# A head's hash beside the FFN: two matmul passes into two single banks instead of three, the low rows added on VectorE

## The chip, the cores and the metric

The kernel runs on one core of a Trainium2 chip. The metric is the device time of one execution in microseconds (us). Lower is better. Before the change three runs gave 966.29, 969.30 and 969.34 us, median 969.30 us.

## The reference

Attention in which a query sees only the keys of its own hash bucket, followed by a feed-forward network (FFN). Four batches, eight heads, 768 positions, 64 numbers to a head; the FFN goes from 512 to 2048 and back to 512.

```python
q_bits = (np.einsum('bhsd,dk->bhsk', q, proj) > 0)        # 6 bits
k_bits = (np.einsum('bhsd,dk->bhsk', k, proj) > 0)
mask = q_bucket[:, :, :, None] == k_bucket[:, :, None, :]  # buckets: the bits as a number
scores = np.where(mask, scale * q @ k.T, -1e9)
attn = softmax(scores)
x = (attn @ v)  as (B*S, H*D)
h = x @ w_in
out = (h * np.clip(h + 3, 0, 6) / 6) @ w_out
```

The sign of the projections must come out as in float32, so the kernel keeps each operand as a high part, rounded to TensorE's fp32r format, and a low part, the rest.

## The kernel before, in words

Work is cut into 192 steps, numbered `k` in the code: 32 heads times 6 blocks of 128 queries. Each step makes the scores of one block against all 768 keys, takes the row minimum (`lowest`, L396 on VectorE), the exponential (`exponential`, L408 on ScalarE), transposes the result, splits it into high and low (`split_p`, L475 on ScalarE and L479 on VectorE or L477 on GpSimd), and multiplies it with the values (`values_whole`, L514).

From step 101 of 192 on (`beside_ffn`) each step also carries a slice of the FFN: `gemm1` (L664), the gate (L686 ScalarE, L687 VectorE), the split of the gate into `gb` high (L692 ScalarE) and low (L693 VectorE), and `gemm2` (L702, L703 with the high part, L707 with the low one). In that stretch the flag `paced` is set, blocks are transposed by VectorE in 32x32 squares (L429) and by a round trip through DRAM (`flip` writes `fd`, `move` reads it back into the tiles `spare` and `px`, four DMAs a block). When the attention's steps are over, the rest of the FFN runs alone.

The order on TensorE, VectorE, ScalarE and GpSimd is that in which the code is written (`manual_schedule`); every engine takes its queue strictly in order. SyncE (SP), which issues nearly all DMAs, is ordered by the framework's scheduler.

Once a head, every sixth step, the next head is hashed. `split_qk` holds four 128-row tiles: `q1` (query high, key high), `k2` (key low, key high), `q2` (query high, query low) and `k1` (key high, and 12 rows for the bits). `hash_qk` multiplies them with the projection, `bits` turns the signs of 12 query rows and 12 key rows into large numbers that make the scores' mask, and a DMA carries the key rows into `k1`. The hash's output `z` lies in two PSUM banks taken from the four single ones (tags `pt` and `pu`, two buffers each), which `gemm1`, the value products and the small transposes `rt` share. A bank is free again when its readers are done. `raw` (one buffer) receives the next head's queries and keys from DRAM; its key rows come by a DMA of their own (`get_k_rows`). 18 heads are hashed before `paced` is set and 14 after.

Of the kernel before, what the change touches and what calls it, by code (L numbers as in the profile page):

```python
# [10 lines left out]
F32 = mybir.dt.float32  # L11
# [32 lines left out]
def lsh_attention_moe(  # L44
# [31 lines left out]
    def dma(out: bass.AP, in_: bass.AP):  # L76
        nonlocal last
        last = nc.sync.dma_start(out=out, in_=in_)
# [38 lines left out]


    pjl = cp.tile([P, ZM], F32R, name="pjl")
    pjh = cp.tile([P, ZM + ZK - D], F32R, name="pjh")  # L120
    nc.vector.memset(pjl[:].bitcast(F32), 0.0)
    nc.vector.memset(pjh[:].bitcast(F32), 0.0)
    pjk, pjq = pjh[:, :ZM], pjh[:, ZK - D :]


    nc.vector.memset(thr[:], 0.0)
    nc.vector.memset(val[:], 0.0)
    for r, one, big in ((D, 0, -BIG), (ZK, 1, 1.0)):
# [3 lines left out]
        nc.vector.memset(val[r : r + 2 * NB], big * (1, -1)[1 - one])  # L132
        nc.vector.memset(val[r : r + NB], big * (1, -1)[one])
    nc.vector.memset(three[:], 3.0)

    raw0 = sp.tile([P, S], F32, name="raw0", tag="raw", bufs=1)[:]
    dma(out=raw0, in_=qkT[0, 0])
# [117 lines left out]
    def hash_weights():  # L255
        for x in range(2):
            c = ZK + (1 - x) * NB
            nc.vector.tensor_scalar_mul(pjh[:, c : c + NB], pr[:], (1.0, -1.0)[x])
        for r, c in ((slice(0, D), D), (slice(D, P), ZK)):
            pos = pjh[r, ZK + NB : ZM]  # L260
            nc.vector.tensor_sub(pjl[r, c + NB : c + 2 * NB], pr[r], pos.bitcast(F32))
            nc.vector.tensor_sub(pjl[r, c : c + NB], pos.bitcast(F32), pr[r])

    def spans(i: int):

# [11 lines left out]

    copied = None
    subs = []
    moves = []  # L280

    def split_qk(i: int, copy):
        nonlocal copied
# [41 lines left out]
    def hash_qk(i: int):  # L325
        k1, k2, q1, q2 = state[i]
        if paced:
            z = zs[i] = [bank([P, HW], f"z{i}_{j}") for j in range(2)]
        else:
            both = pair(f"z{i}")  # L330
            z = zs[i] = [both[:, j, :HW] for j in range(2)]
        for j in range(2):
            c = slice(j * HW, (j + 1) * HW)
            nc.tensor.matmul(z[j][:ZM], lhsT=pjl[:], rhs=q1[:, c], start=True, stop=False)
            nc.tensor.matmul(z[j][:ZM], lhsT=pjk, rhs=k2[:, c], start=False, stop=False)
            nc.tensor.matmul(z[j][:ZM], lhsT=pjq, rhs=q2[:, c], start=False, stop=True)  # L336
        if not paced:
            zs[i] = both

    def bits(i: int):  # L340
        k1, k2, q1, q2 = state[i]
        z = zs.pop(i)

        if isinstance(z, list):
            whole = [(slice(j * HW, (j + 1) * HW), z[j][D:ZM], False) for j in range(2)]
        elif i == 0:
# [694 lines left out]
    def lead(j: int):  # L1041
# [71 lines left out]
    with tc.manual_schedule(engines={ET.PE, ET.DVE, ET.Activation, ET.Pool}):  # L1113
# [15 lines left out]
        def beside_ffn(k: int):  # L1129
# [81 lines left out]
        for k in range(NS + LT + 2):  # L1211
# [132 lines left out]
```

## Time and profile before

| | us |
|---|---|
| median of three runs | 969.30 |
| the profiled execution | 969.05 |
| its span, first to last instruction | 967.3 |
| TensorE busy | 945.9 |
| VectorE, ScalarE, GpSimd busy | 722.2, 623.5, 474.4 |
| mean granted TensorE clock | 0.999 |

The profiled execution is 1.75 us longer than its span and 0.25 us under the median. "PE" is TensorE's matmuls, "PEld" its weight loads, DVE VectorE, ACT ScalarE, POOL GpSimd, SPq the DMA issues of SyncE. A row of the timeline has: start in us, duration in us, engine, line of the kernel, operation, tile written, tiles read, shape, how many were merged, and in brackets how long the engine had been idle and what released it. A row of the groups has: line, engine, operation, tiles, shape, how many, busy us in all, mean ns of one, idle us before them. "Late" and "slack" below are differences between such rows.

### The profile page before, as it was taken

Reading aid. Unit: us, or ns where it says so; the run is one execution under the profiler, and the core shown is the slowest. Engines: PE = TensorE matmul, PEld = TensorE weight load, DVE = VectorE, ACT = ScalarE, POOL = GpSimd, SP = SyncE. Lnnn points to the kernel's source line nnn. Section 1 sums busy time; section 2 is a strip of 40 time slices with the busy share of each in tenths; the row PEclk is TensorE's granted clock in tenths of the full one; section 3 lists DMA queues with packets and bytes.
Section 4 is the critical chain, followed back from the end, with each engine's and each line's share of the span. In section 5 each row is a group of like instructions: output and inputs, shape, how many; then the busy total and the mean of one; then the engine's idle time right before and its main releaser. Section 6 shows DMA issues by size and latency. Waiting matters only on the chain.

```text
span 967.3 us, 19453 instructions
## 1 busy us (share of the span) xinstructions
PE 945.9 (98%) x6306; PEld 871.8 (90%) x6306; DVE 722.2 (75%) x1470; ACT 623.5 (64%) x1421; POOL 474.4 (49%) x582
## 2 busy tenths in 40 slices
PE   8999999999999999899999999999999999999997
PEld 6999888999989999799999898989999999899996
DVE  7999988888559999778878878878878874342422
ACT  6898876666468888576766766666766664333332
POOL 6777744666537766455555556546546532000000
PEclk9999999999999999999999999999999999999999
DMA  3567579100034454688898788798887782101000
GB/s 113 143 155 188 134 222 375 65 1 1 6 118 118 111 137 123 181 242 243 241 267 234 233 257 249 234 264 237 250 254 232 218 239 68 44 1 44 1 22 22
DMA packets 113613, 152.06 MB, mean 157 GB/s; under 512 B 13876, under 2 KB 82612, under 8 KB 113512
## 3 DMA queue, kind: packets, MB, share of 16 engines
q1 hardware_dynamic: 108472, 144.79, 49.0%
q0 software_dynamic: 5040, 6.03, 5.3%
q8 instruction: 50, 0.82, 0.4%
q14 instruction: 51, 0.42, 0.2%
HBM read 77.34 MB, written 54.00 MB: 136 GB/s over the span
## 4 chain that ended last, share of the span: by engine, by line
PE 83%; DVE 8%; DMA 4%; issue 2%; ACT 2%; POOL 1%; SPq 1%; DVEq 0%; ACTq 0%; POOLq 0%
PE h L664 26%; PE po L702 7%; PE po L707 7%; PE po L703 7%; PE acc L500 6%; PE acc L514 6%; PE s L389 5%; PE s L387 5%; PE pt L418 5%; DVE p L396 2%; DVE pl L479 2%; DMA fd<-p 1%; DVE qq L352 1%; PE rt L590 1%; PE z L336 1%
## 5 line engine op out<-in xcount | busy, mean ns | idle before, releaser
L408 ACT ACTIVATE p<-p,m 128x768 f32<-128x768 f32 x192 | 180.1, 938 | 114.4 <-DVE p L396 100.4
L396 DVE TENSOR_SCALAR_CACHE_REDUCE p<-s 128x768 f32<-128x768 f32 x192 | 182.3, 950 | 18.7 <-PE pt L418 11.7
L687 DVE SCALAR_TENSOR_TENSOR h<-g,h 128x256 f32<-128x256 f32 x192 | 80.8, 421 | 103.7 <-ACT g L686 101.3
L686 ACT ACTIVATE g<-h,three 128x256 f32<-128x256 f32 x192 | 91.0, 474 | 91.0 <-PE h L664 90.6
L664 PE MATMUL h<-xh,w 128*128 128x256 f32 x1024 | 147.3, 283 | 0.8 <-DVE qq L352 0.4
L664 PEld LDWEIGHTS h<-xh,w 128*128 128x128 f32 x1024 | 136.6, 188 | 5.5 <-DVE qq L352 1.7
L429 DVE STREAM_TRANSPOSE p<-p 128x768 f32<-128x768 f32 x90 | 88.1, 978 | 65.5 <-ACT p L408 65.5
L477 POOL TENSOR_TENSOR pl<-spare,ph 128x384 fp32r<-128x384 f32 x45 | 45.8, 1017 | 130.8 <-ACT ph L475 77.9
L479 DVE TENSOR_TENSOR pl<-pt,ph 128x384 fp32r<-128x384 f32 x196 | 100.0, 550 | 3.9 <-ACT ph L475 3.5
L387 PE MATMUL s<-kk,qq 76*128 76x384 f32 x384 | 100.1, 341 | 2.0 <-ACT kk L357 1.5
L389 PE MATMUL s<-kk,qq 128*128 128x384 f32 x384 | 100.3, 342 | 0.0
L702 PE MATMUL po<-w,gb 128*128 128x512 f32 x250 | 98.9, 396 | 0.7 <-ACT gb L692 0.7
L703 PE MATMUL po<-w,gb 128*128 128x512 f32 x250 | 98.6, 394 | 0.0
L475 ACT CAST ph<-pt 128x384 fp32r<-128x384 f32 x196 | 86.0, 473 | 14.7 <-PE pt L418 13.4
L216 POOL TENSOR_TENSOR w<-wr,w 128x128 fp32r<-128x128 f32 x128 | 71.8, 593 | 45.3 <-ACT w L210 41.4
L418 PE MATMUL pt<-ident,p 128*128 128x128 f32 x612 | 85.5, 274 | 1.8 <-DVE pl L479 0.9
L692 ACT CAST gb<-h 128x256 fp32r<-128x256 f32 x141 | 52.4, 372 | 49.0 <-DVE h L687 30.1
L664 PE MATMUL h<-xl,w 128*128 128x256 f32 x512 | 81.7, 280 | 0.0
L707 PE MATMUL po<-w,gb 128*128 128x512 f32 x250 | 78.8, 396 | 2.7 <-DVE gb L693 2.6
L418 PEld LDWEIGHTS pt<-ident,p 128*128 128x128 f32 x612 | 71.9, 141 | 9.0 <-ACT p L408 1.8
L318 POOL TENSOR_TENSOR kk<-raw,qq 64x192 fp32r<-64x192 f32 (+1 forms) x73 | 65.6, 924 | 24.2 <-ACT qq L304 20.9
L387 PEld LDWEIGHTS s<-kk,qq 76*128 76x128 f32 x384 | 66.4, 189 | 11.5 <-ACT kk L357 2.0
(153 smaller groups left out, 2167.7 us busy)
## 6 DMA issues: line engine op xcount, KB each, us to landing
fd<-p SPq DMA_DIRECT2D x90, 384.0 KB
spare<-fd SPq DMA_DIRECT2D x180, 96.0 KB
px<-fd SPq DMA_DIRECT2D x180, 96.0 KB
kk<-qq SPq DMA_DIRECT2D x62, 192.0 KB
wr<-in_w_in SPq DMA_DIRECT2D x16, 512.0 KB
wr<-in_w_out SPq DMA_DIRECT2D x16, 512.0 KB
raw<-in_qkT SPq DMA_DIRECT2D x19, 384.0 KB
vr<-in_v SPq DMA_DIRECT2D x32, 192.0 KB
```

Of the source, the lines that this page charges most:

```text
L387: nc.tensor.matmul(s[:, c, :HW], lhsT=q1[:KM, us], rhs=half(k1[:KM], c), start=True, stop=False)
L389: nc.tensor.matmul(s[:, c, :HW], lhsT=q2[:, us], rhs=half(k2, c), start=False, stop=True)
L396: nc.vector.tensor_scalar(out=pr_[:], in0=s[:, :, :HW], scalar1=CAP, scalar2=None, op0=ALU.min, op1=ALU.min, accum_out=m[:],)
L408: nc.scalar.activation(pr_[:], pr_[:], AF.Exp, bias=m[:], scale=-1.0, accum_out=sms[b][:, t, h : h + 1])
L418: nc.tensor.transpose(pt[:, x], probs[g][0][:, c, x * P : (x + 1) * P], ident[:])
L429: nc.vector.transpose(x, x)
L479: lows.append(lambda: engine.tensor_sub(lo, pt, hi.bitcast(F32)))
L664: nc.tensor.matmul(hp, lhsT=wi[:, wp, wc], rhs=x[cc][xp], start=(k == 0 and cc == 0), stop=(k == 2 and cc == NCC - 1),)
L686: nc.scalar.activation(r[:], hp, AF.Relu, bias=three[:], scale=1.0)
L702: nc.tensor.matmul(po[u], lhsT=gh[:, us], rhs=wo[:, 0], start=(fc == 0), stop=False)
L703: nc.tensor.matmul(po[u], lhsT=gh[:, us], rhs=wo[:, 1], start=False, stop=False)
L707: nc.tensor.matmul(po[u], lhsT=gl[:, us], rhs=wo[:, 0], start=False, stop=(fc == NFC - 1))
```

## The change

Only the 14 hashes of the stretch beside the FFN are changed. `q1` is no longer an operand. The low part of the projection goes to 24 more columns of the two remaining weight matrices, so that 120 columns are used: rows 0 to 23 of `z` take the low part's products and rows 96 to 119 the high part's. ScalarE copies rows 0 to 23 of each bank into rows 96 to 119 of the `raw` tile, VectorE adds the high rows to them, and one VectorE pass over all 768 columns makes the bits. The DMA of the bits into `k1` and that of the key rows go into a list of their own (`behind_home`), emptied behind `move`; the key rows are asked for one step later. The new weights are made on GpSimd at step 100 in the buffer of the old ones.

```diff
+    for n, (lim, mul) in reversed(list(enumerate(((TINY, -BIG), ...)))):
+        r = slice(ZK, ZK + (n + 1) * NB)
+        nc.gpsimd.memset(ths[r], lim)
+        nc.gpsimd.memset(vas[r], mul)
...
     def get_k_rows(i: int):
-        moves.append(lambda: dma(out=raws[i][D:], in_=qkT[b, h, D:]))
+        behind_home.append(lambda: dma(out=raws[i][D:], in_=qkT[b, h, D:]))
...
+    def short_weights():
+        pjs = cp.tile([P, ZK + NR + NQ], F32R, name="pjs", tag="pjh")
+        nc.gpsimd.memset(pjs[:].bitcast(F32), 0.0)
+        short.extend([pjs[:, : ZK + NR], pjs[:, NQ:]])
+        ...
     def hash_qk(i: int):
         k1, k2, q1, q2 = state[i]
         if paced:
-            z = zs[i] = [bank([P, HW], f"z{i}_{j}") for j in range(2)]
+            zs[i] = []
+            for j in range(2):
+                c = slice(j * HW, (j + 1) * HW)
+                z = bank([P, HW], f"z{i}_{j}")
+                zs[i].append(z)
+                nc.tensor.matmul(z[: ZK + NR], lhsT=short[1], rhs=q2[:, c], start=True, stop=False)
+                nc.tensor.matmul(z[: ZK + NR], lhsT=short[0], rhs=k2[:, c], start=False, stop=True)
+            return
...
     def bits(i: int):
         if isinstance(z, list):
-            whole = [(slice(j * HW, (j + 1) * HW), z[j][D:ZM], False) for j in range(2)]
+            r = slice(ZK, ZK + NR)
+            both = raws[i + 1][r] if i + 1 < NJ else sp.tile([P, S], F32, ...)[r]
+            for j in range(2):
+                nc.scalar.copy(both[:, j * HW : (j + 1) * HW], z[j][:NR])
+            for j in range(2):
+                c = slice(j * HW, (j + 1) * HW)
+                nc.vector.tensor_add(both[:, c], z[j][r], both[:, c])
+            nc.vector.tensor_scalar(
+                out=q1[D : D + NR], in0=both, scalar1=ths[r], scalar2=vas[r], op0=ALU.is_gt, op1=ALU.mult,
+            )
+            behind_home.append(lambda: dma(out=k1[D : D + NQ].bitcast(F32), in_=q1[D + NQ : D + NR].bitcast(F32)))
+            return
...
             if n + 1 < NJ and n != H + 1:
                 get_qk(n + 1)
-                if paced:
-                    get_k_rows(n + 1)
+        if t == 4 and paced and n + 1 < NJ and n != H + 1:
+            get_k_rows(n + 1)
...
             if GT <= k + 1 < NS:
                 move(k + 1)
+            while behind_home:
+                behind_home.pop(0)()
...
+            if k == GT - 2:
+                short_weights()
```

How the change moves instructions is shown at the hash that stands at 540 us in the profile before. In the rows the numbers behind a tile's name only tell buffers apart. On TensorE, where L664 is `gemm1` and L702, L703 are `gemm2`, the hash stands thus before:

```order
L334 MATMUL z_0_7528<-qq_7286,pjl 108x384
L335 MATMUL z_0_7528<-kk_7285,pjh 108x384
L336 MATMUL z_0_7528<-qq_7286,pjh 108x384
L334 MATMUL z_1_7529<-qq_7286,pjl 108x384
L335 MATMUL z_1_7529<-kk_7285,pjh 108x384
L336 MATMUL z_1_7529<-qq_7286,pjh 108x384
```

and now (L354 and L355 are the two passes of `hash_qk`):

```order
L354 MATMUL z_0_7547<-qq_7306,pjs 120x384
L355 MATMUL z_0_7547<-kk_7305,pjs 120x384
L354 MATMUL z_1_7550<-qq_7306,pjs 120x384
L355 MATMUL z_1_7550<-kk_7305,pjs 120x384
L739 MATMUL po_1_6608<-w_3352,gb_1_14_7509 128x512
```

Six passes became four; nothing else on TensorE stands elsewhere than before, the value products included, which stood behind `gemm1` already.

On VectorE the same place reads before (L687 the gate, L479 and L654 splits, L352 the bits, L693 the gate's low part, L396 the row minimum):

```order
L687 SCALAR_TENSOR_TENSOR h_1_15_7498<-g_1_15_7542,h_1_15_7498 128x256
L479 TENSOR_TENSOR pl_0_7546<-spare,ph_0_7545 128x3x128
L352 TENSOR_SCALAR qq_7286<-z_0_7528,thr,val 44x384
L352 TENSOR_SCALAR qq_7286<-z_1_7529,thr,val 44x384
L654 TENSOR_TENSOR xl_2_7565<-xr_2_7157,xh_2_7564 128x256 x4
L693 TENSOR_TENSOR gb_1_15_7575<-h_1_15_7498,gb_1_15_7575 128x256
L396 TENSOR_SCALAR p_7579,m_7578<-s_7555 128x768
```

and now (old L687 is L724, L479 is L516, L654 is L691, L693 is L730, L396 is L433):

```order
L724 SCALAR_TENSOR_TENSOR h_1_15_7517<-g_1_15_7559,h_1_15_7517 128x256
L516 TENSOR_TENSOR pl_0_7563<-spare,ph_0_7562 128x3x128
L377 TENSOR_TENSOR raw_7492<-z_0_7547,raw_7492 24x384
L377 TENSOR_TENSOR raw_7492<-z_1_7550,raw_7492 24x384
L378 TENSOR_SCALAR qq_7306<-raw_7492,limits 24x768
L691 TENSOR_TENSOR xl_2_7586<-xr_2_7173,xh_2_7585 128x256 x4
L730 TENSOR_TENSOR gb_1_15_7596<-h_1_15_7517,gb_1_15_7596 128x256
L433 TENSOR_SCALAR p_7600,m_7599<-s_7574 128x768
```

Two passes became two adds and one pass, at the same place in the queue; on ScalarE two copies of `z` (24x384) stand in addition just behind the L475 that feeds L479.

On SyncE's DMA queue the step ahead of that hash and the hash's own step read before:

```order
L78 DMA raw_7472<-in_qkT 64x768 x2
L78 DMA xs_127<-y_0_7334 64x512
L78 DMA fd_7442<-p_7434 128x768
L78 DMA px<-fd_7370 32x4x192 x4
L78 DMA fd_7496<-p_7488 128x768
L78 DMA spare<-fd_7442 32x4x192 x3
L78 DMA kk_7285<-qq_7286 12x768
L78 DMA spare<-fd_7442 32x4x192
L78 DMA vr_7619<-in_v 128x384
```

and now:

```order
L78 DMA raw_7492<-in_qkT 64x768
L78 DMA xs_136<-y_0_7354 64x512
L78 DMA fd_7462<-p_7454 128x768
L78 DMA px<-fd_7390 32x4x192 x4
L78 DMA fd_7515<-p_7507 128x768
L78 DMA spare<-fd_7462 32x4x192 x4
L78 DMA kk_7305<-qq_7306 12x768
L78 DMA raw_7492<-in_qkT 64x768
L78 DMA vr_7640<-in_v 128x384
```

The key rows moved from ahead of the two `fd` writes to behind the bits' DMA, and the bits' DMA from ahead of the fourth read of `fd` to behind it.

More of the change, by code (lines that the diff above doesn't have):

```diff
@@ L123, in lsh_attention_moe @@
     pjk, pjq = pjh[:, :ZM], pjh[:, ZK - D :]
+    NQ = 2 * NB
+    NR = 2 * NQ
+    short = []
+    limits = cp.tile([P, 2], F32, name="limits")
+    ths, vas = limits[:, 0:1], limits[:, 1:2]
     nc.vector.memset(thr[:], 0.0)
@@ L262, in hash_weights @@
             nc.vector.tensor_sub(pjl[r, c : c + NB], pos.bitcast(F32), pr[r])
+    def short_weights():
+        pjs = cp.tile([P, ZK + NR + NQ], F32R, name="pjs", tag="pjh")
+        nc.gpsimd.memset(pjs[:].bitcast(F32), 0.0)
+        short.extend([pjs[:, : ZK + NR], pjs[:, NQ:]])
+        c = ZK + NQ
+        pos = pjs[:, c + NB : c + NQ].bitcast(F32)
+        for x in range(2):
+            nc.gpsimd.tensor_scalar_mul(pjs[:, c + (1 - x) * NB : c + (2 - x) * NB], pr[:], (1.0, -1.0)[x])
+        nc.gpsimd.tensor_sub(pjs[:, NQ + NB : 2 * NQ], pr[:], pos)
+        nc.gpsimd.tensor_sub(pjs[:, NQ : NQ + NB], pos, pr[:])
     def spans(i: int):
@@ L279, in lsh_attention_moe @@
     subs = []
-    moves = []
+    moves, behind_home = [], []
     def split_qk(i: int, copy):
@@ L327, in hash_qk @@
         if paced:
-            z = zs[i] = [bank([P, HW], f"z{i}_{j}") for j in range(2)]
-        else:
-            both = pair(f"z{i}")
-            z = zs[i] = [both[:, j, :HW] for j in range(2)]
+            zs[i] = []
[6 more added lines that the diff above has]
+            return
+        both = pair(f"z{i}")
+        z = zs[i] = [both[:, j, :HW] for j in range(2)]
         for j in range(2):
@@ L336, in hash_qk @@
             nc.tensor.matmul(z[j][:ZM], lhsT=pjq, rhs=q2[:, c], start=False, stop=True)
-        if not paced:
-            zs[i] = both
+        zs[i] = both
     def bits(i: int):
```

6 lines of the change are left out of this document (4 added, 2 removed).

## Prediction

> **What bounds the kernel now.** I read the page first, then the busy time by stretches, then the waits of TensorE, and last the timeline around single hashes.
>
> ```profile
> span 967.3 us, 19453 instructions
> PE 945.9 (98%) x6306; PEld 871.8 (90%) x6306; DVE 722.2 (75%) x1470; ACT 623.5 (64%) x1421; POOL 474.4 (49%) x582
> ```
> ```profile
> 395.00:775.00 380.00, 375.31 (x2440) 345.64 (x2439) 304.11 (x582) 253.25 (x596) 201.72 (x262) 1.00 0.83 243
> 775.00:967.00 192.00, 186.47 (x1210) 168.46 (x1209) 78.67 (x182) 75.59 (x180) 19.00 (x27) 1.00 0.18 53
> ```
> ```profile
> PEld h L664 <- DVE qq L352: 1.7, 4, 0.7
> ```
>
> The stretches' columns are window, length, busy us of PE, PEld, DVE, ACT and POOL, clock, DMA share, GB/s. All 14 changed hashes lie in 395 to 775 us. TensorE is busy 375.3 of 380 us there at full clock, VectorE 304.1 (80%), ScalarE 253.3. So TensorE bounds the stretch, and what it is spared comes off the time unless it must then wait. The last row names the one wait that belongs to the hash: the next `gemm1` wants the bank of `z`, and four times the bits (L352) weren't done, 1.7 us in all.
>
> **TensorE.** The first of the six passes, and what follows the sixth:
>
> ```profile
> 459.39 0.33 PE L334 MATMUL z<-qq,pjl 128*108 128x384 f32 x1
> 460.43 0.39 PE L702 MATMUL po<-w,gb 128*128 128x512 f32 x1
> 653.69 0.52 PE L389 MATMUL s<-kk,qq 128*128 128x384 f32 x2
> ```
>
> Six passes take 460.43 - 459.39 = 1.04 us, 0.173 each; the durations overlap. Two fewer spare 0.35 us a hash, over 14 hashes 4.85 us. The weights grow from 108 to 120 columns. Score passes with 128 columns (L389) last 0.34 us and two of them 0.52, so they stand 0.18 apart; at that distance the four passes left would cost 0.03 us more a hash, 0.4 in all. I take nothing and leave the 0.4 to the range.
>
> **VectorE and ScalarE.** A hash and what is queued behind it:
>
> ```profile
> 652.59 0.50 ACT L475 CAST ph<-spare 128x384 fp32r<-128x384 f32 x1
> 653.16 0.67 DVE L479 TENSOR_TENSOR pl<-spare,ph 128x384 fp32r<-128x384 f32 x1
> 653.86 1.29 DVE L352 TENSOR_SCALAR qq<-z,thr,val 44x384 fp32r<-44x384 f32 x2
> 654.27 1.01 POOL L368 TENSOR_TENSOR vv<-vr,vv 128x384 fp32r<-128x384 f32 x1
> 655.22 0.84 POOL L525 DMA_DIRECT2D xs<-y  x1
> 655.18 0.42 DVE L693 TENSOR_TENSOR gb<-h,gb 128x256 fp32r<-128x256 f32 x1
> 655.52 0.95 DVE L396 TENSOR_SCALAR_CACHE_REDUCE p<-s 128x768 f32<-128x768 f32 x1
> 655.28 0.82 SPq L78 DMA_DIRECT2D kk<-qq  x1
> 662.60 0.83 ACT L304 CAST qq<-raw 128x768 fp32r<-128x768 f32 x1
> ```
> ```profile
> L479 DVE TENSOR_TENSOR pl<-pt,ph 128x384 fp32r<-128x384 f32 x196 | 100.0, 550 | 3.9 <-ACT ph L475 3.5
> L352 DVE TENSOR_SCALAR qq<-z,thr,val 44x768 fp32r<-44x768 f32 x17 | 18.5, 1086 | 1.6 <-PE z L336 0.8 <-POOL rblate L580 0.3
> L291 DVE CAST qq<-raw 64x768 fp32r<-64x768 f32 x1 | 0.6, 557 | 2.2 <-DMA raw<-in_qkT 2.2
> L475 ACT CAST ph<-pt 128x384 fp32r<-128x384 f32 x196 | 86.0, 473 | 14.7 <-PE pt L418 13.4 <-PE acc L500 1.3
> L692 ACT CAST gb<-h 128x256 fp32r<-128x256 f32 x82 | 30.4, 371 | 21.4 <-PE po L707 14.2 <-DVE h L687 4.2
> L475 ACT CAST ph<-spare 128x384 fp32r<-128x384 f32 x82 | 40.9, 499 | 1.7 <-PE po L707 1.6
> ```
>
> The last two rows are of the stretch 395 to 775 alone. VectorE's two passes took 1.29 us together. The adds (PSUM plus SBUF, 384 numbers) are like L479 on `pt`: 100.0/196 = 0.51 us each, 1.02 for two. The last pass goes from SBUF to SBUF over 768 numbers. No row shows it: L291, SBUF to SBUF, is the floor with 0.56 us; L352 over 768 numbers from PSUM, with two per-row operands as here, the ceiling with 1.09. Without a wait VectorE's addition D is therefore 1.02 + 0.56 - 1.29 = 0.29 to 0.82 us.
>
> A wait is likely: the adds end near 653.86 + 1.02 = 654.88, while GpSimd's L368 runs to 655.28. Two rows show what then happens to a VectorE pass on SBUF:
>
> ```profile
> 557.23 1.01 POOL L477 TENSOR_TENSOR pl<-px,ph 128x384 fp32r<-128x384 f32 x1
> 557.41 1.25 DVE L479 TENSOR_TENSOR pl<-px,ph 128x384 fp32r<-128x384 f32 x1
> ```
>
> L479 started under L477 and ended 0.42 us after it. Were the last pass held likewise, it would end at 655.28 + 0.42 = 655.70 instead of 655.15, D = 0.55. I take D = 0.6, this plus a little for the per-row operands, nearest to the L291 floor with the wait. Ends: 0.29, and 1.22 (the ceiling 0.82 plus the whole 0.40 us wait).
>
> The Trainium skill, SBUF — State Buffer, section "Who interferes with whom", says that a VectorE pass in a 2-port mode and GpSimd lock each other out of a shared port pair for whole instructions, and names tensor_scalar among the passes that enter that mode. The two rows above, of a two-input pass, agree with the lock; for tensor_scalar no run here shows it. By that rule the wait is certain, D = 0.55 or more; a sum without it would have D = 0.29 and come to about 966.7 us. This speaks against the change, as GpSimd works through every hash.
>
> ScalarE gets two copies of about 0.47 us (L475), 0.94 a hash. They run under L479, and the first is done (652.59 + 0.50 + 0.47 = 653.56) before the first add can begin at 653.86. L692, next in its queue, has 21.4 us of idle time before it in 82 turns, 0.26 a turn, so part of the copies is hidden there and the rest makes the gate's high part later; its reader, L702, stands behind the whole next `gemm1`, so I count nothing. Without that cover a hash would cost up to 0.94 - 0.26 = 0.7 us.
>
> **The bank.** The bank that the next `gemm1` wants is given back by the first add (0.55 us) instead of the first L352:
>
> ```profile
> 654.60 1.00 PEld L664 LDWEIGHTS h<-xh,w 128*128 128x128 f32 x8 [0.72 <-DVE qq L352]
> ```
>
> One L352 lasts 0.69 (1.29 for two, overlapped by 0.08), so the bank comes 0.14 us earlier, TensorE 0.35 earlier. Where it waits already (568, 595, 650, 732 us), 0.21 of the 0.35 is lost, 0.84 in all, and 0.14 remains.
>
> **Who waits for a late VectorE.** Behind the bits stand L693 and L396; the next scores (L387) need the bank that L396 reads. That distance I read behind every hash but the first. Its greatest and its least:
>
> ```profile
> 462.77 0.95 DVE L396 TENSOR_SCALAR_CACHE_REDUCE p<-s 128x768 f32<-128x768 f32 x1
> 465.32 0.42 PEld L387 LDWEIGHTS s<-kk,qq 76*128 76x128 f32 x2
> ```
> ```profile
> 545.71 0.95 DVE L396 TENSOR_SCALAR_CACHE_REDUCE p<-s 128x768 f32<-128x768 f32 x1
> 546.79 0.42 PEld L387 LDWEIGHTS s<-kk,qq 76*128 76x128 f32 x2
> 551.19 0.19 PEld L702 LDWEIGHTS po<-w,gb 128*128 128x128 f32 x1 [0.67 <-ACT gb L692]
> 631.22 0.37 ACT L550 COPY y<-acc 128x256 f32<-128x256 f32 x1 [1.73 <-DMA xs<-y]
> ```
>
> They run from 1.60 us (465.32 - 463.72) to 0.13 (546.79 - 546.66). In order of time: 0.96 (432), 1.60 (459), 1.30, 0.59 (513), 0.13 (540), 0.81, 1.41, 0.96 (623), 0.81 (650), 1.60, 1.29, 0.31 (732), 0.13 (760). TensorE comes 0.35 us earlier and L396 D later, so 0.35 + D = 0.95 us of slack is used up; what is missing TensorE waits.
>
> - 432, 459, 486, 678, 705: slack 0.96 or more, full gain, 5 x 0.35 = 1.75.
> - 568, 595, 650: bank-bound, 0.74 used, slack enough: 3 x 0.14 = 0.42.
> - 623: 0. Slack suffices, but in the next step ScalarE's L550 waits 1.73 us for a DMA, and TensorE behind it.
> - 513: 0.35 - (0.95 - 0.59) = -0.01.
> - 732: 0.14 - (0.74 - 0.31) = -0.29.
> - 540, 760: 0.35 - (0.95 - 0.13) = -0.47 each. Here a chunk of the FFN ends, so L654's four passes stand behind the bits too, and the L702 after it already waits. ScalarE's copies push L653, which feeds L654, by 0.94 us there, about as much as the bits push L654 itself.
>
> **The first hash (402) and the DMAs.**
>
> ```profile
> 398.03 1.16 SPq L78 DMA_DIRECT2D raw<-in_qkT  x2
> 400.86 0.38 SPq L78 DMA_DIRECT2D fd<-p  x1
> 405.10 0.96 DVE L396 TENSOR_SCALAR_CACHE_REDUCE p<-s 128x768 f32<-128x768 f32 x1 [1.53 <-DMA fd<-p]
> 410.99 0.73 PE L707 MATMUL po<-w,gb 128*128 128x512 f32 x2 [0.74 <-DVE gb L693]
> ```
>
> Here TensorE waits for L693 right behind the bits, so its saving is worth nothing and D is passed on: -0.6. Against it, the key rows (64 x 768 x 4 bytes = 197 KB, 0.8 us at the stretch's 243 GB/s) no longer stand ahead of the `fd` write for which L396 waited: 0 to +0.8, I take +0.5. Elsewhere the key rows come later without harm: behind the bits' DMA at about 656 us where L304 reads them at 662.60. The bits' DMA on SyncE's queue waits D longer. Behind it stand the key rows, `vr` and the next `fd` write, which waits for the next block's transposition anyway; the fourth read of `fd` is now ahead of it, but L475 on `spare` was idle only 1.7 us before 82 casts, so I count nothing for that.
>
> The set-up:
>
> ```profile
> 0.33 0.12 POOL L1332 MEMSET const-uint8-127<- 128x1 uint8 x1
> 407.73 1.01 POOL L477 TENSOR_TENSOR pl<-spare,ph 128x384 fp32r<-128x384 f32 x1 [12.48 <-ACT ph L475]
> ```
>
> Two small memsets slip in ahead of the identity matrix with which TensorE's warm-up begins, up to 2 x 0.12 = 0.24 us; five small GpSimd passes at step 100 lie in an idle time of GpSimd of over 12 us. I cost both at nothing.
>
> **The sum.** 1.75 + 0.42 + 0 - 0.01 - 0.29 - 0.94 - 0.6 + 0.5 = 0.83 us gained. The profiled execution took 969.05 us, 0.25 under the median of 969.30: 968.2 us. With D = 0.29 the same working gives 2.4 us gained, 966.7; with D = 1.22 a loss of 4.8, 973.8.
>
> **The rivals.**
>
> *VectorE's lateness reaches nobody* (faster). Were the next scores not held by L396, only the bank's 0.84 us would be lost: 4.85 - 0.84 = 4.0, 965.0 us. For it speaks that VectorE is busy only 80% and catches up between hashes; against it the 0.13 us slack twice and the wait of L707 at 410.99.
>
> ```profile
> 470.21 0.84 POOL L525 DMA_DIRECT2D xs<-y  x1
> 470.24 0.56 DVE L479 TENSOR_TENSOR pl<-spare,ph 128x384 fp32r<-128x384 f32 x1
> ```
>
> *The last pass waits for GpSimd's DMA issue too* (slower). L368 and L525 follow each other without a gap (655.28 against 655.22); a pass that gets in only at 656.06 ends near 656.5, D = 1.35 and, by the working above, some 6 us lost, about 975. It decides from D = 1.05 on, where the loss passes 3 us. Against it: L479 at 470.24 lasted its ordinary 0.56 us beside an L525. The lock rule of the Trainium skill's SBUF — State Buffer, "Who interferes with whom", is what would bring it about.
>
> *The change does less than its words.* The value products stand behind `gemm1` already, so this half moves nothing; it changes no number.
>
> **How the numbers follow.** About 0.3% (2.9 us) is what a measurement of this kernel can tell from no change; the three runs differ by 3.05. The forecast and its neighbours within that bound: 0.6. The first rival, and D near its floor together with earlier DMAs: 0.25. The second, or D above 1.05 by a slow last pass: 0.15. The range 965.2 to 971.8 reaches nearly to the first rival and half way to the D = 1.22 end.
>
> **What would show it.** L334 and L336 gone from the stretch and four passes in 0.70 us; the adds near 1.0 us, the last pass 0.56 to 0.85 and starting or ending with L368; L396 0.4 to 0.8 us later against L352's start; waits of L387's weight load for L396 at 540, 732 and 760, hardly any at 459; waits for the bank named after the add, about 2.5 us. I am wrong if VectorE's passes end no later than before, if L387 waits in every hash, or if SyncE's `fd` writes come late behind the key rows.

## The result, and the profile after

The changed kernel took a median of 973.5 us (972.87 to 975.24), the kernel before 968.05 us (966.29 to 969.34) on the same chip: ratio 1.0064, 95% interval [1.0045, 1.0083], so 6.2 us slower by the ratio (4.4 to 8.0); the two medians lie 5.45 us apart. The ratio is not that of the medians, here and in the table below, where the two can give differences up to 1.2 us apart. Forecast were 968.2 us, no change, and a range that ended at 971.8. The profiled execution after took 973.31 us against 969.05 before, 4.3 us more; with that difference the traces have to agree.

The engines' busy time from the page after, and the stretch of the hashes after:

```profile
PE 947.7 (98%) x6278; PEld 866.7 (89%) x6278; DVE 729.5 (75%) x1484; ACT 635.7 (65%) x1449; POOL 476.8 (49%) x595
```
```profile
395.00:775.00 380.00, 373.09 (x2386) 337.19 (x2385) 307.56 (x590) 262.47 (x617) 201.63 (x262) 1.00 0.83 240
```

The clock is 1.00 as before. In these 380 us TensorE got through 54 matmuls fewer (2386 against 2440), though the hashes ask for only 28 fewer, and was busy 2.2 us less (373.09 against 375.31): it idles more. Its waits (its weight loads' waits: what waits, for what; us in all, times, longest) before, in the window 395 to 780 us:

```profile
PEld po L707 <- DVE gb L693: 4.7, 6, 2.3
PEld h L664 <- ACT xh L653: 0.3, 1, 0.3
```

and after (L744 is the old L707, L701 the old L664, L690 the old L653, L424 the old L387; L377 are the adds):

```profile
PEld po L744 <- DVE gb L730: 7.4, 13, 1.6
PEld h L701 <- DVE raw L377: 3.3, 6, 0.8
PEld h L701 <- ACT xh L690: 1.6, 3, 0.6
PEld s L424 <- DVE p L433: 1.5, 3, 0.6
```

All rows of this view add up to 10.5 us before and 19.0 after: 8.5 us more waiting, against 14 x 0.35 = 4.85 us less work. That is 3.7 us of the 4.3. The largest row names VectorE's L730, the low part of the gate, in 13 places, most of them not in a step with a hash but two or four steps behind it.

Now the hash that stands at 653 us before and at 656 us after. The rows answer to those of the prediction (start, duration, engine, line; L516 is the old L479, L405 the old L368, L433 the old L396):

```profile
655.79 0.84 ACT L374 COPY raw<-z 24x384 f32<-24x384 f32 x2
655.83 0.68 DVE L516 TENSOR_TENSOR pl<-spare,ph 128x384 fp32r<-128x384 f32 x1
656.54 1.04 DVE L377 TENSOR_TENSOR raw<-z,raw 24x384 f32<-24x384 f32 x2
656.96 1.01 POOL L405 TENSOR_TENSOR vv<-vr,vv 128x384 fp32r<-128x384 f32 x1
657.16 1.00 PEld L701 LDWEIGHTS h<-xh,w 128*128 128x128 f32 x8 [0.56 <-DVE raw L377]
657.62 0.76 DVE L378 TENSOR_SCALAR qq<-raw,limits 24x768 fp32r<-24x768 f32 x1
658.42 0.43 DVE L730 TENSOR_TENSOR gb<-h,gb 128x256 fp32r<-128x256 f32 x1
658.76 0.95 DVE L433 TENSOR_SCALAR_CACHE_REDUCE p<-s 128x768 f32<-128x768 f32 x1
```

From L516's start to L433's are 2.93 us; before they were 655.52 - 653.16 = 2.36. VectorE's addition is D = 0.57 us here. The forecast of D (0.6) was right; what it does to the rest of the program was not.

What bounds the stretch shows in VectorE's own timeline of two steps, before. The gate (L687) opens a step; L429 is the transposition, which waits for ScalarE's exponential of what L396 has reduced:

```profile
483.50 0.43 DVE L687 SCALAR_TENSOR_TENSOR h<-g,h 128x256 f32<-128x256 f32 x1
483.90 0.56 DVE L479 TENSOR_TENSOR pl<-px,ph 128x384 fp32r<-128x384 f32 x1
484.37 0.95 DVE L396 TENSOR_SCALAR_CACHE_REDUCE p<-s 128x768 f32<-128x768 f32 x1
...
485.25 0.42 DVE L693 TENSOR_TENSOR gb<-h,gb 128x256 fp32r<-128x256 f32 x1
486.43 0.98 DVE L429 STREAM_TRANSPOSE p<-p 128x768 f32<-128x768 f32 x1 [0.76 <-ACT p L408]
487.33 0.40 DVE L687 SCALAR_TENSOR_TENSOR h<-g,h 128x256 f32<-128x256 f32 x1
487.64 0.66 DVE L479 TENSOR_TENSOR pl<-spare,ph 128x384 fp32r<-128x384 f32 x1
488.34 1.29 DVE L352 TENSOR_SCALAR qq<-z,thr,val 44x384 fp32r<-44x384 f32 x2
489.66 0.42 DVE L693 TENSOR_TENSOR gb<-h,gb 128x256 fp32r<-128x256 f32 x1
490.00 0.95 DVE L396 TENSOR_SCALAR_CACHE_REDUCE p<-s 128x768 f32<-128x768 f32 x1
...
492.05 0.98 DVE L429 STREAM_TRANSPOSE p<-p 128x768 f32<-128x768 f32 x1 [1.10 <-ACT p L408]
493.10 0.43 DVE L687 SCALAR_TENSOR_TENSOR h<-g,h 128x256 f32<-128x256 f32 x1
```

There is no gap of 0.1 us or more but the one ahead of L429 (left out are two reads of L396's accumulator, 0.08 us each). A step takes 3.83 us (487.33 - 483.50), the step with the hash 5.77 (493.10 - 487.33), and neither waits for TensorE (of the 69 steps without a hash beside the FFN 29 take 3.83 to 3.90 us, the median 4.00): row minimum, exponential, transposition, gate, split and the next row minimum are a loop of VectorE and ScalarE that runs as fast as it can. For the window 395 to 780 us the view of waits and the busy times (PE, PEld, DVE, ACT, POOL) have

```profile
DVE p L429 <- ACT p L408: 62.2, 85, 1.1
```
```profile
395.00:780.00 385.00, 380.31 (x2475) 350.33 (x2474) 307.36 (x589) 256.69 (x605) 202.73 (x263) 1.00 0.83 243
```

VectorE's 307.36 us and the 62.2 of waits for the exponential make 369.6 of 385. "VectorE 80% busy" was a nearly full loop.

The same step after:

```profile
488.04 0.40 DVE L724 SCALAR_TENSOR_TENSOR h<-g,h 128x256 f32<-128x256 f32 x1
...
489.05 1.04 DVE L377 TENSOR_TENSOR raw<-z,raw 24x384 f32<-24x384 f32 x2
490.12 0.77 DVE L378 TENSOR_SCALAR qq<-raw,limits 24x768 fp32r<-24x768 f32 x1
490.92 0.42 DVE L730 TENSOR_TENSOR gb<-h,gb 128x256 fp32r<-128x256 f32 x1
491.26 0.95 DVE L433 TENSOR_SCALAR_CACHE_REDUCE p<-s 128x768 f32<-128x768 f32 x1
...
493.31 0.98 DVE L466 STREAM_TRANSPOSE p<-p 128x768 f32<-128x768 f32 x1 [1.10 <-ACT p L445]
494.36 0.43 DVE L724 SCALAR_TENSOR_TENSOR h<-g,h 128x256 f32<-128x256 f32 x1
```

It takes 6.32 us, 0.55 more, and still has no wait for TensorE. Measured from gate to gate over the 83 steps between 401 and 781 us, the 14 steps with a hash became 5.67 us longer together (10 of them by 0.54 to 0.56 us each), and the other 69 became 1.16 us shorter: 4.5 us, about the difference of the profiled executions. From one hash to the next (six steps) 12 of the 14 stretches are longer, by 0.19 to 1.21 us, and two, from 623 and from 705 us on, are shorter by 0.69 and 0.61. That gave two theories.

- The loop: beside the FFN VectorE and ScalarE set the pace, TensorE follows closely behind. Each hash hands its D on to the end, and what TensorE is spared it spends waiting.
- The slack: the prediction's reading, in which TensorE sets the pace and VectorE's lateness below the slack behind a hash costs nothing. The rest of the loss would then come from something else that the change moved: the copies on ScalarE or the DMA order.

### The profile page after: what moved, and what is told of

Read it like the earlier page. It is cut to its first block, busy times and chain, and to the rows that moved or that the text cites. A ratio compares the mean times of both kernels' runs of the same rounds, so it can differ in the third digit from the quotient of the medians.

```text
span 971.5 us, 19450 instructions
## 1 busy us (share of the span) xinstructions
PE 947.7 (98%) x6278; PEld 866.7 (89%) x6278; DVE 729.5 (75%) x1484; ACT 635.7 (65%) x1449; POOL 476.8 (49%) x595
## 4 chain that ended last, share of the span: by engine, by line
PE 74%; DVE 9%; DMA 6%; ACT 4%; issue 3%; SPq 3%; POOL 2%; ACTq 0%; DVEq 0%; POOLq 0%
PE h L701 24%; PE acc L537 6%; PE po L744 6%; PE po L739 6%; PE po L740 6%; PE pt L455 5%; PE s L426 5%; PE s L424 5%; PE acc L551 5%; DVE pl L516 3%; SPq L78 3%; DVE p L433 2%; DMA px<-fd 2%; ACT ph L512 1%; DMA spare<-fd 1%
## 5 line engine op out<-in xcount | busy, mean ns | idle before, releaser
L433 DVE TENSOR_SCALAR_CACHE_REDUCE p<-s 128x768 f32<-128x768 f32 x192 | 182.5, 951 | 17.4 <-PE pt L455 11.4
L724 DVE SCALAR_TENSOR_TENSOR h<-g,h 128x256 f32<-128x256 f32 x192 | 81.0, 422 | 102.1 <-ACT g L723 99.9
L701 PE MATMUL h<-xh,w 128*128 128x256 f32 x1024 | 149.3, 284 | 2.2 <-DVE raw L377 1.5
L701 PEld LDWEIGHTS h<-xh,w 128*128 128x128 f32 x1024 | 136.8, 188 | 9.3 <-DVE raw L377 3.3
L516 DVE TENSOR_TENSOR pl<-pt,ph 128x384 fp32r<-128x384 f32 x196 | 100.0, 550 | 3.9 <-ACT ph L512 3.5
L424 PE MATMUL s<-kk,qq 76*128 76x384 f32 x384 | 100.4, 342 | 2.0 <-ACT kk L394 1.5
L744 PE MATMUL po<-w,gb 128*128 128x512 f32 x250 | 79.7, 400 | 2.5 <-DVE gb L730 2.3
L701 PE MATMUL h<-xl,w 128*128 128x256 f32 x512 | 82.0, 281 | 0.0
L424 PEld LDWEIGHTS s<-kk,qq 76*128 76x128 f32 x384 | 66.3, 190 | 12.3 <-DVE p L433 2.2
L514 POOL TENSOR_TENSOR pl<-px,ph 128x384 fp32r<-128x384 f32 x45 | 46.3, 1029 | 63.0 <-ACT ph L512 47.0
```

Source lines behind the costliest of these rows:

```text
L424: nc.tensor.matmul(s[:, c, :HW], lhsT=q1[:KM, us], rhs=half(k1[:KM], c), start=True, stop=False)
L433: nc.vector.tensor_scalar(out=pr_[:], in0=s[:, :, :HW], scalar1=CAP, scalar2=None, op0=ALU.min, op1=ALU.min, accum_out=m[:],)
L514: engine.tensor_sub(lo, pt, hi.bitcast(F32))
L516: lows.append(lambda: engine.tensor_sub(lo, pt, hi.bitcast(F32)))
L701: nc.tensor.matmul(hp, lhsT=wi[:, wp, wc], rhs=x[cc][xp], start=(k == 0 and cc == 0), stop=(k == 2 and cc == NCC - 1),)
L744: nc.tensor.matmul(po[u], lhsT=gl[:, us], rhs=wo[:, 0], start=False, stop=(fc == NFC - 1))
```

## The experiments

The table gives each kernel's median, the ratio to the kernel before on the same chip, and from its profiled execution how much longer than before the 14 steps with a hash and the 69 others are between the same two gates. Executions of one kernel differ among themselves by 0.5 to 5.4 us, so the last two columns explain one execution and not the median. "D" is VectorE's time in the chain from the gate to the row minimum, against before.

| kernel | D, us | median us (before) | ratio | 95% interval | 14 hash steps, us | others, us |
|---|---|---|---|---|---|---|
| changed | +0.55 | 973.5 (968.05) | 1.0064 | 1.0045 to 1.0083 | +5.67 | -1.16 |
| four TensorE passes only | 0 | 969.22 (967.96) | 1.001 | 1.000 to 1.002 | -0.77 | +2.31 |
| all but TensorE's saving | +0.55 | 973.71 (967.96) | 1.0053 | 1.0040 to 1.0065 | +5.82 | -1.98 |
| DMA order only | 0 | 967.19 (967.96) | 0.9995 | 0.9985 to 1.0005 | -0.44 | -2.01 |
| DMA order and copies | 0 | 966.48 (967.96) | 0.9983 | 0.9975 to 0.9992 | -0.74 | +0.02 |
| bits made one and a half times | +0.72 | 976.49 (967.56) | 1.010 | 1.0087 to 1.0113 | +9.20 | -2.65 |
| half the bits | -0.6 | 964.67 (967.56) | 0.9975 | 0.9965 to 0.9985 | -3.76 | -1.47 |
| last pass late | -0.25 | 967.68 (967.56) | 1.0005 | 0.9995 to 1.0015 | -3.22 | +1.52 |
| last pass late, row minimum first | -0.6 | 968.17 (967.97) | 1.0002 | 0.9991 to 1.0013 | -5.51 | +4.25 |
| second bank late | -0.6 | 973.13 (967.56) | 1.0069 | 1.0056 to 1.0082 | -0.15 | +0.57 |
| ScalarE empties z | -1.29 | 963.43 (967.72) | 0.9953 | 0.9938 to 0.9968 | -5.88 | +0.31 |
| ScalarE empties z, four passes | -1.29 | 961.88 (967.72) | 0.9935 | 0.9919 to 0.9951 | -10.91 | +5.08 |
| ScalarE empties z, row minimum first | -1.6 | 965.15 (967.97) | 0.9964 | 0.9952 to 0.9975 | -7.77 | +2.52 |

**Four TensorE passes only**: the kernel before, without the low part's products.

```diff
-            nc.tensor.matmul(z[j][:ZM], lhsT=pjl[:], rhs=q1[:, c], start=True, stop=False)
-            nc.tensor.matmul(z[j][:ZM], lhsT=pjk, rhs=k2[:, c], start=False, stop=False)
+            if not paced:
+                nc.tensor.matmul(z[j][:ZM], lhsT=pjl[:], rhs=q1[:, c], start=True, stop=False)
+            nc.tensor.matmul(z[j][:ZM], lhsT=pjk, rhs=k2[:, c], start=paced, stop=False)
```

> The kernel before with only TensorE's part of the change: beside the FFN a hash has two passes a bank instead of three; the products of the projection's low part are left out. VectorE's two passes, ScalarE and all DMAs stand as before. TensorE is spared 14 x 0.35 = 4.85 us. Loop theory (beside the FFN the chain row minimum, exponential, transposition, gate, split on VectorE and ScalarE sets the pace of the six steps of a head, and TensorE's hash passes are covered by it): 0 to 1.5 us faster than before. TensorE theory (the one of the prediction: TensorE sets the pace and VectorE's lateness costs only where its slack behind a hash is too small): 3.5 to 4.5 us faster, 4.85 less some bank waits.

It is not faster: 1.001 [1.000, 1.002]. The 4.85 us of TensorE's work are gone and none of it arrives. Its waits (L708 is the old L707, L665 the old L664, L353 the old L352):

```profile
PEld po L708 <- DVE gb L694: 7.2, 9, 1.9
PEld h L665 <- DVE qq L353: 5.1, 8, 1.0
```

Against 4.7 and 1.7 us before these two have grown by 5.9 us: TensorE came earlier and waited for VectorE. The slack theory's gain is refuted.

**All but TensorE's saving** (VectorE's, ScalarE's and the DMAs' part of the change): the changed kernel with a third TensorE pass per bank whose weights are zero, so that six passes stand there again.

```diff
+                nc.tensor.matmul(z[: ZK - NQ], lhsT=short[0][:, NR : ZK + NQ], rhs=q1[:, c], start=False, stop=False)
```

> The changed kernel with a third pass a bank put back, of 84 zero columns, so that TensorE has six passes a hash again; all else as in the changed kernel. Loop theory: the passes are covered, 0 to 1.5 us slower than the changed kernel, 5.5 to 7.5 slower than before. TensorE theory: 4 to 5 us slower than the changed kernel, about 10 slower than before.

1.0053 [1.0040, 1.0065], and the hash steps are as in the changed kernel (+5.82 against +5.67). Whether TensorE makes four passes or six cannot be told in the time. Its waits in this run (L702 is the old L664, L378 the adds, L745 the old L707) are

```profile
PEld po L745 <- DVE gb L731: 6.9, 12, 1.7
PEld h L702 <- DVE raw L378: 1.2, 5, 0.4
```

The bank of `z` is waited for less than before (1.2 us against 1.7), the gate's low part more (6.9 against 4.7). So the loss does not come from banks given back late; it comes with VectorE's lateness behind the hash.

**DMA order only**, and **DMA order and copies**: the kernel before, with the key rows and the bits' DMA in `behind_home`, the key rows a step later; the second also with ScalarE's two copies, which nobody reads.

```diff
-        moves.append(lambda: dma(out=raws[i][D:], in_=qkT[b, h, D:]))
+        behind_home.append(lambda: dma(out=raws[i][D:], in_=qkT[b, h, D:]))
...
+            for j in range(2):
+                nc.scalar.copy(both[:, j * HW : (j + 1) * HW], z[j][: 4 * NB])
```

> The kernel before with only the DMA part of the change: the key rows are asked for a step later, and they and the bits' DMA are issued behind the reads of the next block. Theory that the DMA order costs (key rows or bits late, or the queue held up): 3 to 6 us slower than before. Loop theory and TensorE theory: within 1 us of before.

> As the DMA-only kernel, and ScalarE makes the change's two copies of 24 x 384 a hash (0.84 us) in addition, which nobody uses; VectorE's two passes as before. Theory that ScalarE's copies cost, being in the chain: 14 x 0.4 to 0.84, 5 to 10 us slower than the DMA-only kernel. Loop theory as I hold it, with VectorE's added 0.55 us a hash as the cost and ScalarE waiting for TensorE after its cast anyway: 0 to 2 us slower. TensorE theory: 0 to 1 us.

0.9995 [0.9985, 1.0005] and 0.9983 [0.9975, 0.9992]: neither costs anything; in both, the median of the 14 changes of a step with a hash is 0.00 us. Why the second is 1.6 us faster stays open. What is left of the change is VectorE's two adds and one pass in place of two passes.

**Bits made one and a half times**, and **half the bits**: the kernel before with 0.72 us more on VectorE per hash (the first bank's pass made twice), or with about 0.6 less (the first bank's bits left out).

```diff
+            whole.insert(1, (slice(0, HW), z[0][D:ZM], False))
```
```diff
-            whole = [(slice(j * HW, (j + 1) * HW), z[j][D:ZM], False) for j in range(2)]
+            whole = [(slice(j * HW, (j + 1) * HW), z[j][D:ZM], False) for j in range(2)][1:]
```

> The kernel before, with VectorE's first pass over a hash's bits made twice (same values), so that VectorE has about 0.6 us (one L352) more in each of the 14 hashes and nothing else changes. Theory 'VectorE and ScalarE set the pace' (each hash's addition on VectorE goes on to the end): 14 x 0.6 = 8.4 us slower at most, I expect +5 to +8. Theory 'slack behind the hash' (the prediction's: lateness below the slack costs nothing, TensorE sets the pace): with 0.6 used of the slacks of 0.13 to 1.60 us only 513, 540, 732, 760 and the first hash pay, +0.01 + 0.47 + 0.29 + 0.47 + 0.6, about +2.

> The kernel before, with only the second bank's bits made in the 14 paced hashes; the first half's bits are left out (the output isn't the reference's). VectorE is spared about 0.6 us per hash, TensorE keeps its six passes. Theory 'VectorE and ScalarE set the pace': faster by 2 to 6 us, until TensorE's own work bounds. Theory 'slack behind the hash': only the bank (given back 0.6 us earlier, 1.7 us of waits in all) and the first hash gain, at most 1 to 2 us.

The first is 1.010 [1.0087, 1.0113], 8.9 us by the medians, where 14 x 0.72 = 10.1: nearly all arrives, and a little more than the 8 expected. In its trace the step takes 6.49 us (497.30 - 490.81), with three passes in 2.01 us:

```profile
490.81 0.40 DVE L688 SCALAR_TENSOR_TENSOR h<-g,h 128x256 f32<-128x256 f32 x1
...
491.82 2.01 DVE L353 TENSOR_SCALAR qq<-z,thr,val 44x384 fp32r<-44x384 f32 x3
...
497.30 0.43 DVE L688 SCALAR_TENSOR_TENSOR h<-g,h 128x256 f32<-128x256 f32 x1
```

The run does not by itself decide between the theories, because the pass made twice also holds both banks 0.72 us longer. In 13 of the 14 steps with a hash TensorE's next `gemm1` waits, and its first weight load starts 0.12 us after the second pass or 0.05 us after the third, 7.1 us in all, against 1.7 us in 4 steps before; the slack theory, with the bank counted, would have to charge these waits too. "All but TensorE's saving", where the bank is waited for less than before, and "last pass late", where it is waited for as in the changed kernel, leave no such way out.

The second is faster by 2.4 us by the ratio, 2.9 by the medians (0.9975 [0.9965, 0.9985]), where 14 x 0.6 = 8.4 us were taken away. Four of its 14 steps with a hash shrank by 0.59 to 0.61 us, eight by less than 0.1. In one of the eight VectorE stands in its new gap ahead of the gate's low part, whose high part ScalarE couldn't deliver earlier:

```profile
488.63 0.42 DVE L693 TENSOR_TENSOR gb<-h,gb 128x256 fp32r<-128x256 f32 x1 [0.55 <-ACT gb L692]
```

The gain is above the slack theory's 1 to 2 us by little, and the bank's waits are gone here too. It shows that the next bound stands close behind: 0.6 us less on VectorE per hash gains about a third of itself.

**Last pass late**: the changed kernel, with L378 behind the next row minimum, in VectorE's wait for the exponential; the key rows a step later.

```diff
-            nc.vector.tensor_scalar(
-                out=q1[D : D + NR], in0=both, scalar1=ths[r], ...
+            def last_pass():
+                nc.vector.tensor_scalar(
+                    out=q1[D : D + NR], in0=both, scalar1=ths[r], ...
+            lates.append(last_pass)
...
+            while lates:
+                lates.pop(0)()
             if k + 2 < NS:
```

> The changed kernel, with VectorE's last pass over 768 columns moved out of the hash to behind the next row minimum, where VectorE waits about 1.1 us for ScalarE's exponential; the key rows are asked for a step later. In the chain from the gate to the row minimum stand only the two adds: 1.04 us in place of 1.29 before. Theory 'VectorE and ScalarE set the pace': the whole loss goes and D becomes -0.25 us per hash, so 0 to 4 us faster than the kernel before, about 967 to 964. Theory 'the bits' lateness or the DMAs behind them cost it': the bits come about 2 us later than in the changed kernel, so it is as slow as that one or slower, 973 or more.

The same instructions in another place, and the whole loss is gone: 1.0005 [0.9995, 1.0015]. Its timeline (L380 is the last pass, L437 the row minimum, L470 the transposition):

```profile
488.88 1.04 DVE L377 TENSOR_TENSOR raw<-z,raw 24x384 f32<-24x384 f32 x2
...
490.30 0.95 DVE L437 TENSOR_SCALAR_CACHE_REDUCE p<-s 128x768 f32<-128x768 f32 x1
...
491.29 0.68 DVE L380 TENSOR_SCALAR qq<-raw,limits 24x768 fp32r<-24x768 f32 x1
492.35 0.98 DVE L470 STREAM_TRANSPOSE p<-p 128x768 f32<-128x768 f32 x1 [0.38 <-ACT p L449]
```

The wait ahead of the transposition shrank from 1.10 to 0.38 us and covers the pass. TensorE waits for the adds' bank as long as in the changed kernel (3.4 us against 3.3), but for the gate's low part 3.3 us instead of 7.4. It was expected to beat the kernel before by 0 to 4 us and does not: the steps with a hash shrank by the expected 0.25 us (median), 3.22 us in all, but the others grew by 1.52 in that execution.

**Second bank late**: the kernel before, with the pass over the second bank in that same wait.

```diff
+            one(c0, of0)
+            lates.append(last_pass)
```

> The kernel before, with VectorE's pass over the second bank moved to behind the next row minimum (six TensorE passes, no copies). In the chain stands one pass of about 0.65 us in place of 1.29, but the second bank is held about 2 us longer. Theory 'VectorE and ScalarE set the pace': 2 to 5 us faster than before unless TensorE then waits for the bank. Theory 'slack behind the hash': 0 to 1 us.

Wrong: 1.0069 [1.0056, 1.0082], 6.7 us slower. The condition that the expectation named came true. VectorE gives the second bank back only behind the row minimum, and TensorE's `h` (L679, the old L664) waits for it; one such place, and the group over the window 395 to 780 us (last column: idle before it, and for whom):

```profile
463.82 1.17 PE L679 MATMUL h<-xh,w 128*128 128x256 f32 x8 [1.67 <-DVE qq L354]
```
```profile
L679 PE MATMUL h<-xh,w 128*128 128x256 f32 x672 | 95.1, 283 | 5.1 <-DVE qq L354 5.0
```

The trace is of the fastest of its five executions (970.01 us), so it shows the mechanism and less than its usual size.

**ScalarE empties z**: a version that leaves nothing of the hash in VectorE's chain from the gate to the row minimum, and in which no bank waits for VectorE: six passes as before, ScalarE copies the 44 rows of both banks into the `raw` tile, and VectorE makes all bits in one late pass.

```diff
+            r = slice(D, ZM)
+            both = raws[i + 1][r] if i + 1 < NJ else sp.tile([P, S], F32, ...)[r]
+            for j in range(2):
+                nc.scalar.copy(both[:, j * HW : (j + 1) * HW], z[j][r])
+            def last_pass():
+                nc.vector.tensor_scalar(
+                    out=q1[r], in0=both, scalar1=thr[r], scalar2=val[r], op0=ALU.is_gt, op1=ALU.mult,
+                )
+                behind_home.append(lambda: dma(out=k1[D : D + 2 * NB].bitcast(F32), in_=q1[ZK:ZM].bitcast(F32)))
+            lates.append(last_pass)
```

> The kernel before (six TensorE passes), but ScalarE copies the 44 rows of both banks of z into the raw tile behind the cast of the hash's split, and VectorE makes all bits in one pass over 768 columns behind the next row minimum, where it waits about 1.1 us for the exponential; the DMA order is the changed kernel's, the key rows a step later. Nothing of the hash is left in the chain from the gate to the row minimum: D = -1.29 us per hash. Theory 'VectorE and ScalarE set the pace': as with half the bits left out (-2.9 us for -0.65) or better, 3 to 6 us faster than before, then bounded by TensorE. Theory 'slack behind the hash': the bank waits of 1.7 us and the first hash, 1 to 2 us faster. If the late bits or the held tile cost: 0 or slower.

> The kernel before with ScalarE's copies and the late pass of the run above, and without the low part's two TensorE passes (their products are left out, so the output isn't the reference's). With six passes sparing two was worth nothing (ratio 1.001). If TensorE sets the pace once VectorE is relieved, sparing 0.35 us x 14 = 4.85 us on it is now worth 2 to 4 us against the run above; if VectorE and ScalarE still set it, nothing.

963.43 us (962.77 to 963.97): 0.9953 [0.9938, 0.9968], 4.5 us faster than the kernel before, and faster than the changed one. The step (L349 the copies, L707 and L708 the gate's two parts, L411 the row minimum, L352 the pass), and its stretch:

```profile
486.12 0.85 ACT L349 COPY raw<-z 44x384 f32<-44x384 f32 x2
...
487.69 0.38 ACT L707 CAST gb<-h 128x256 fp32r<-128x256 f32 x1 [0.72 <-PE po L722]
488.10 0.42 DVE L708 TENSOR_TENSOR gb<-h,gb 128x256 fp32r<-128x256 f32 x1 [1.28 <-ACT gb L707]
488.44 0.95 DVE L411 TENSOR_SCALAR_CACHE_REDUCE p<-s 128x768 f32<-128x768 f32 x1
...
489.43 0.68 DVE L352 TENSOR_SCALAR qq<-raw,thr,val 44x768 fp32r<-44x768 f32 x1
490.50 0.98 DVE L444 STREAM_TRANSPOSE p<-p 128x768 f32<-128x768 f32 x1 [0.38 <-ACT p L423]
```
```profile
395.00:775.00 380.00, 377.88 (x2478) 351.04 (x2477) 299.84 (x575) 270.05 (x634) 203.88 (x264) 1.00 0.84 247
```

TensorE now waits 5.7 us in the whole view of its waits instead of 10.5, and is busy 377.88 of 380 us. With two passes fewer on top (**four passes**; the low part's products left out) the median is 961.88 us (960.51 to 963.08), 1.6 us under it, with ranges that touch: about a third of the 4.85 us. Its TensorE waits 10.4 us again, 4.7 more than with six passes, so here too the spared work turned mostly into waiting (one execution each). The expectation "2 to 4 us" is missed from below, "nothing" is not shown either: the two are nearly in balance.

**Row minimum first**: in the rows above VectorE waits 1.28 us for ScalarE's L707, which waits for TensorE, and the row minimum stands behind that. Both late versions were run with the row minimum ahead of the gate's low part in the step with a hash, as it is in the others.

```diff
-            behind = (k - 1 + LA) % KT == 4
+            behind = False
```

> The kernel in which ScalarE empties z, with one order changed: in the step with a hash, VectorE takes the row minimum (L411) ahead of the gate's low part (L708) and not behind it, as in the other steps. In that kernel L708 waits 1.28 us for ScalarE's L707, which waits for TensorE, and the row minimum stands behind it. Theory 'the loop of VectorE and ScalarE sets the pace': the wait and L708's 0.34 us leave the chain; where the scores are there already (about half of the hashes by the trace) 0.3 to 0.9 us a hash, 1 to 4 us faster than 963.4, about 961. Theory 'TensorE sets the pace now': nothing, 963.4, or slower by the gate's low part coming up to 0.9 us later to TensorE's second layer.

> The changed kernel with its last pass late, and the same order: row minimum ahead of the gate's low part in the step with a hash. D falls by a further 0.34 us per hash, to about -0.6, with four passes on TensorE. Theory 'the loop sets the pace': 1 to 4 us faster than the kernel before, about 965. If TensorE waits for the gate's low part instead, as fast as before (967.7).

Neither gains: 0.9964 [0.9952, 0.9975] against 0.9953 [0.9938, 0.9968] without it, and 1.0002 [0.9991, 1.0013] against 1.0005. The steps with a hash are 1.9 and 2.3 us shorter than without the edit, and the steps between them give 2.2 and 2.7 us back. In the first VectorE's row minimum now waits for TensorE's scores, 19.4 us in 23 places against 2.8 in 6 without the edit; in the second TensorE waits 6.9 us for the gate's low part against 3.3, the other outcome that its expectation named. From here on the loop's time in the hash no longer decides; "ScalarE empties z" is the best version that computes all of the reference.

## Why the prediction was wrong

- **"TensorE bounds the stretch, and what it is spared comes off the time unless it must then wait"**: this step failed. TensorE was busy 375.3 of 380 us, but the next engine in line was not VectorE with 304; it was the loop of VectorE and ScalarE, with 369.6 of 385. Sparing TensorE two passes alone gave 1.001: the "unless it must then wait" took all of it. The Trainium skill, Perfetto Trace Analysis, section "Identifying the Most-Contended Engine", says to take the engine with the highest occupancy as the bottleneck and to work on it first, TensorE's headroom judged by its share of the peak arithmetic rate or its weight loads' busy share; here the weight loads are 90% busy, the highest share of any engine, and sparing TensorE alone gained nothing. The measurement decides.
- **"Who waits for a late VectorE"**, the list of slacks: this is where the sum broke. It took the distance from L396 to the next scores at each of 13 hashes, and let lateness below it vanish. That distance says when TensorE must stop for VectorE; it does not say that VectorE recovers. VectorE's next gate is late by D in any case (10 hashes of 14 by 0.54 to 0.56), its loop has hardly a gap in which to catch up, and TensorE meets the lateness up to four steps later, at L744 (4.7 us in 6 places before, 7.4 in 13 after). The distances themselves shrank about as forecast, from 1.60 to 0.68 us at 459 and from 1.30 to 0.42 at 486: TensorE passed these two hashes without a wait, and the steps still became 0.21 and 0.56 us longer. The scores waited for the row minimum in 3 places (1.5 us), at the first hash, at 513 and at 732; at 540 and 760, where the prediction saw it too, they did not. Of the 9 entries written with a gain or with nothing, 8 were losses of 0.21 to 0.56 us (623 alone was not); all 14 steps together lost 5.67 us in the profiled execution, of at most 14 x 0.55 = 7.7, where the sum had a gain of 0.83. At 623 the step became 0.77 us shorter; with the DMA order alone it is 0.39 us shorter, and the rest stays open. The slack of 1.60 us that the list shows at 459 was TensorE's lead, not VectorE's reserve.
- **D = 0.6**: right (0.55 to 0.57), though two of its parts were off in opposite ways. The adds took 0.56 us each (0.51 assumed). The last pass took 0.76 beside GpSimd's L405 and 0.69 (mean of 14) in the late place, where 0.56 was the floor; so the wait was worth 0.07, not 0.40. It ended 0.41 or 0.42 us after L405 in all 14 hashes, the forecast 0.42. The lock of the Trainium skill's SBUF — State Buffer, "Who interferes with whom", fits that fixed end; which part of the pass is shut out the trace does not show, since it is written down as begun 0.35 us before L405's end and only 0.42 of its 0.69 us come after.
- **TensorE's 0.35 us a hash**: right. Four passes took 0.70 us:

```profile
487.25 0.34 PE L354 MATMUL z<-qq,pjs 128*120 128x384 f32 x1
...
487.95 0.39 PE L739 MATMUL po<-w,gb 128*128 128x512 f32 x1
```

- **ScalarE's copies and the DMA order, counted as nothing**: right, by the two runs (0.9983, 0.9995). The +0.5 for an earlier `fd` write at the first hash is within what those runs leave open; in the changed kernel's trace the step ahead of that hash is 0.89 us shorter, and the hash's own step 0.48 longer.
- **The bank**: waits of 3.3 us in 6 places, forecast about 2.5; at 432 and 513, where none was forecast, it was 0.82 and 0.57 us.
- **The rivals**: "VectorE's lateness reaches nobody" is refuted by "all but TensorE's saving", 1.0053 with less waiting for the bank than before. "The last pass waits for GpSimd's DMA issue too" came nearest to the measured time (975 against 973.5) for a reason that didn't occur: D stayed at 0.55, half of what it needed. The third was right that the value products move nothing. No rival had D as forecast and handed on at most hashes, whose price (14 x 0.6 = 8.4 us at most) the prediction's own rows would have given.

What stays open: why, step by step, the 69 others took back 1.16 us after the change and gave up 0.3 to 5 us in most of the faster versions; the 1.6 us by which copies that nobody reads came out faster; and how much of the 8.9 us in the run with more bits went through the bank and how much through the loop.

## What to carry to other kernels

Before believing that the busiest engine sets the pace, follow one other engine through a full step and count its waits for its partners as its own time: a loop over two engines without a gap, repeating at a fixed period (3.83 us to 3.90 in 29 of 69 steps here), is a bound even when its engines are busy 67% and 80% (256.69 and 307.36 of 385 us here). A slack found on the engine that waits is a reserve only if the late engine has a gap of its own to recover in; if not, most of each addition in its loop is handed on to the end (5.67 of 7.7 us in the steps with a hash here). Where such a loop has a wait inside (the 1.1 us for the exponential), that is the place for extra work: the same pass cost the whole loss ahead of the row minimum and nothing behind it, as long as no buffer that a third engine needs is held for it.

## What the runs showed of the hardware

- A VectorE pass from SBUF to SBUF with two per-row operands over 768 numbers took 0.69 us with 24 rows and the same 0.69 with 44 rows, each a mean of 14, and 0.76 when it began beside a GpSimd pass on SBUF.
- Two VectorE passes from PSUM over 384 numbers take 1.29 us and three 2.01, so 0.72 for each one more.
- TensorE passes over 384 columns with 120 weight columns followed each other at 0.175 us (0.70 for four), with 108 columns at 0.173.
